# No tensor work on GpSimd: V laid out by head dimension for both pairs, Sinkhorn and P's transposes rearranged

## The chip, the core and the metric

The kernel runs on one core of a Trainium2 chip. The core's engines work in parallel, each through its own instructions in order: TensorE (PE; its weight loads are shown apart as PEld), VectorE (DVE), ScalarE (ACT), GpSimd (POOL) and SyncE (SP, which here only starts DMAs). The metric is the time of one execution on the device, in microseconds (us); lower is better.

## What is computed

Four batches of eight heads, 768 positions, head dimension 64. An 8 x 8 matrix per head is normalised by Sinkhorn steps and mixes the eight blocks of 96 positions of K and V; attention with the mixed K and V follows. Its output goes through a two-dimensional Fourier transform whose real part is added, and through a normalised MLP.

```python
def _attn_ref(q, k, v, sort_net):
    ...
    P = sort_net
    for _ in range(5):
        P = P - np.max(P, axis=-1, keepdims=True)
        P = np.exp(P)
        P = P / (np.sum(P, axis=-1, keepdims=True) + 1e-09)
        P = P / (np.sum(P, axis=-2, keepdims=True) + 1e-09)
    k_b = k.reshape(B, H, n_blocks, block, D)
    v_b = v.reshape(B, H, n_blocks, block, D)
    k_sorted = np.einsum('bhij,bhjcd->bhicd', P, k_b).reshape(B, H, S, D)
    v_sorted = np.einsum('bhij,bhjcd->bhicd', P, v_b).reshape(B, H, S, D)
    ...
    scores = scale * np.matmul(q_b, k_sb.transpose(0, 1, 2, 4, 3))
    scores = scores - np.max(scores, axis=-1, keepdims=True)
    attn = np.exp(scores)
    attn = attn / (np.sum(attn, axis=-1, keepdims=True) + 1e-09)
    return np.matmul(attn, v_sb).reshape(B, H, S, D).astype(np.float32)

def _moe_ref(x, w_ch1, w_ch2):
    X = np.fft.fft(x, axis=1)
    X = np.fft.fft(X, axis=2)
    mixed = np.real(X).astype(np.float32)
    u = x + mixed
    mu = np.mean(u, axis=-1, keepdims=True)
    var = np.mean((u - mu) ** 2, axis=-1, keepdims=True)
    un = (u - mu) / np.sqrt(var + 1e-06)
    ch = np.maximum(un @ w_ch1, 0.0) @ w_ch2
    return (u + ch).astype(np.float32)
```

## The kernel before

The kernel is one list of operations that a planner puts in order. `P.add` records an operation with the engines that may run it and a guessed cost on each, what it reads and writes, and a priority. `schedule` walks a simulated clock: each engine takes the ready operation of lowest priority number; where several engines may run one, the one that is free first takes it. The result is a fixed order on each engine, and an instruction that waits holds everything behind it on its engine. The guesses decide the order alone, not how long anything takes.

Inputs come by DMAs that GpSimd issues (line 395), small tables by SyncE. Sinkhorn (`sk`, lines 493 to 515) is a chain of 32-partition operations on VectorE with one exponential on ScalarE in each of five iterations. VectorE first clears the tiles `eb` and `ks` (437, 441). P is then spread out (`pk` at 517 on VectorE, `pv` at 521 on ScalarE) and transposed on TensorE: for the keys at 530, from which `bdk` is built (535, and `make_bdk` at 551 for later batches), and for the values at 648, from which `bdv` is built (653). The transposes at 648 are eight fp32 matmuls recorded as one operation.

Attention (`attn`) goes over pairs of heads: `q_copy` (771) gathers q into `qr`, `kqt` mixes the keys (786), copies them out to `ks` and transposes q into `qt` (807, 812), `scores` computes scores (830), their exponential into `ex` (839) and the exponential minus one into `eb` (851 on VectorE, 853 on ScalarE; one of three `ex` buffers is held until then), `av` multiplies with the mixed values and normalises (870 to 884). Copies out of PSUM and others go through one helper, `copy`, so many rows carry its line, 560, and are told apart by their tiles.

The values are handled for two pairs of batches, t = 0 and 1. `v_path` sums V over a block on TensorE (575) and makes the mean `vb`/`vbn` on VectorE (582 to 591). For t = 0 four copies of 1536 values (597) put V into the tile `vcx` with the head dimension innermost. `v_mix` then takes, for each of 64 dimensions d, the columns of `vcx` with that d as weights (626, a stride of 64 values) and subtracts the mean with a second matmul (628). For t = 1 GpSimd subtracts the mean in eight operations (607), which write `vcx` with d outermost: neighbours in the order of writing lie 96 values, 192 bytes, apart. The weights of a dimension then lie in a row (632) and no second matmul is needed. The mixed values go from PSUM into `vsf` (640).

`a_path` computes small tables `rr` (689 to 740). `dft1` and `dft2` are the Fourier transform; `y` is copied out of PSUM on ScalarE (941) and `yr`, its reversal, is made on VectorE or GpSimd (947). `dft2` also makes the normalisation, whose small steps at 1015 to 1024 run on GpSimd. `mlp` is the MLP: FF1 at 1067, its ReLU on ScalarE or VectorE (1079, 1076), FF2 at 1088, the sum at 1096, the store at 1099. Attention of a batch and the MLP of an earlier one are interleaved by their priorities.

```python
vcd = vcx[:, 0:6144].rearrange("p (d r c) -> p c r d", r=6, c=16)
for n in range(8):
    P.add({"POOL": (1.7, 1.8)},
          lambda _, n=n: nc.gpsimd.tensor_tensor(
              vcd[:, 2 * n:2 * n + 2],
              n3[:, 12 * n:12 * n + 12, :].rearrange(
                  "p (c r) d -> p c r d", r=6),
              vbn[:, None, None, :].broadcast_to([128, 2, 6, D]),
              op=ALU.subtract),
```

## Time and profile before

| | |
|---|---|
| median of 3 runs | 346.91 us (346.67 to 347.95) |
| the profiled execution | 349.38 us, span of the profile 347.6 us |
| TensorE busy | 287.0 us (83%) |
| VectorE busy | 216.0 us (62%) |
| ScalarE busy | 149.2 us (43%) |
| GpSimd busy | 90.4 us (26%) |
| chain that ended last | PE 66%, DVE 26%, issue 3%, POOL 2%, ACT 2% |

An engine's busy time counts its instructions from start to end, so one that is held up after it has started counts as busy. The span in 40 slices of 8.7 us (busy tenths of each engine):

```profile
PE   0397989777950009998999999999999999999994
DVE  7766889999999994297981559642552423531002
ACT  2364046755840006375892175054174162270520
POOL 8343601534289992000120023000022010010000
```

Rows of the list of groups read: line, engine, operation, out<-in, shapes, count | busy us, mean ns of one | idle before it, and what ended that. Rows of the timeline read: start, length, engine, line, operation, count [idle before it].

### The profile page before, as it was taken

How to read it: one execution, taken by the hardware profiler on the slowest of the kernel's cores; microseconds unless marked ns; L12 is line 12 of the kernel's file. 1: busy time of each engine (PE TensorE's matmuls, PEld its weight loads, DVE VectorE, ACT ScalarE, POOL GpSimd, SP SyncE). 2: the span in 40 equal slices, each digit the busy share in tenths (PEclk: the TensorE clock that was granted, in tenths of full speed). 3: DMA queues.
4: the chain of work that ended last, by engine and by line, in shares of the span. 5: the costliest groups of instructions: out<-in, count | busy, mean ns of one | idle time of the engine just before them, and what ended most of it. 6: DMA issues, size and time to landing. Idle time of an engine off the chain costs nothing.

```text
span 347.6 us, 6040 instructions
## 1 busy us (share of the span) xinstructions
PE 287.0 (83%) x2452; PEld 182.2 (52%) x2452; DVE 216.0 (62%) x404; ACT 149.2 (43%) x304; POOL 90.4 (26%) x103
## 2 busy tenths in 40 slices
PE   0397989777950009998999999999999999999994
PEld 0367978654630005575665566555565565564541
DVE  7766889999999994297981559642552423531002
ACT  2364046755840006375892175054174162270520
POOL 8343601534289992000120023000022010010000
PEclk9996965996995557998999999999999999999999
DMA  8999999630000009010000110100110100201002
GB/s 134 202 284 211 209 211 208 98 52 10 0 2 0 0 1 180 18 46 1 32 2 2 61 42 2 62 30 2 60 42 2 60 32 10 82 2 60 32 0 91
DMA packets 16402, 22.40 MB, mean 64 GB/s; under 512 B 1162, under 2 KB 11928, under 8 KB 16372
## 3 DMA queue, kind: packets, MB, share of 16 engines
q0 software_dynamic: 12144, 15.16, 24.6%
q1 hardware_dynamic: 4230, 6.85, 5.3%
q8 instruction: 19, 0.31, 0.4%
q14 instruction: 9, 0.07, 0.1%
HBM read 28.95 MB, written 6.29 MB: 101 GB/s over the span
## 4 chain that ended last, share of the span: by engine, by line
PE 66%; DVE 26%; issue 3%; POOL 2%; ACT 2%; DVEq 0%
PE bank L1088 24%; PE bank L1067 21%; DVE yr L947 9%; PE bank L870 3%; PE bank L626 3%; PE bank L987 2%; PE bank L786 2%; PE bank L1047 2%; DVE qt L560 1%; PE bank L628 1%; PE bank L575 1%; PE bank L830 1%; PE bank L807 1%; DVE rt L884 1%; PE bank L994 1%
## 5 line engine op out<-in xcount | busy, mean ns | idle before, releaser
L1067 PE MATMUL bank<-ut,w1sb 128*128 128x384 f16 x512 | 94.5, 330 | 0.0
L1079 ACT ACTIVATE hr<-bank 128x384 f16<-128x384 f32 x109 | 53.5, 491 | 85.4 <-PE bank L1067 82.7
L1088 PE MATMUL bank<-w2sb,hr 128*128 128x512 f16 x384 | 88.7, 381 | 0.0
L1067 PEld LDWEIGHTS <-w1sb 128*128 128x128 f16 x512 | 48.6, 99 | 33.9 <-issue 1.8
L1096 DVE TENSOR_TENSOR u<-bank,u 128x512 f32<-128x512 f32 x24 | 16.5, 688 | 70.0 <-PE bank L1088 70.0
L1088 PEld LDWEIGHTS <-hr 128*128 128x128 f16 x384 | 37.1, 98 | 41.3 <-issue 0.3
L839 ACT ACTIVATE ex<-bank 96x384 f32<-96x384 f32 x64 | 28.0, 482 | 55.3 <-DVE eb L851 31.1
L786 PE MATMUL bank<-bdk,kq 128*64 128x128 f16 x192 | 13.6, 261 | 31.6 <-ACT ex L839 30.6
L947 DVE TENSOR_SCALAR yr<-y 128x384 f16<-128x384 f16 x7 | 33.9, 4837 | 0.5 <-ACT y L941 0.5
L1002 DVE SCALAR_TENSOR_TENSOR u<-rt,bank 128x512 f32<-128x512 f16 x24 | 16.1, 679 | 27.9 <-PE bank L994 27.9
L607 POOL TENSOR_TENSOR vcx<-kq,vbn 128x768 f16<-128x768 f16 x8 | 30.7, 4234 | 1.4 <-DVE vbn L588 1.4
L1015 POOL TENSOR_SCALAR mv<-mv 128x3 f32<-128x3 f32 x8 | 3.1, 383 | 102.6 <-DVE mv L1010 102.5
L786 PEld LDWEIGHTS <-kq 128*64 128x64 f16 x192 | 9.1, 129 | 35.4 <-issue 34.4
L853 ACT ACTIVATE eb<-ex,negone 96x384 f16<-96x384 f32 x37 | 21.9, 612 | 0.3
L870 PE MATMUL bank<-vsf,eb 97*128 97x65 f16 x384 | 18.0, 207 | 1.5 <-issue 0.9
L560 DVE CAST vsf<-bank 96x512 f16<-96x512 f32 x22 | 16.6, 781 | 3.8 <-PE bank L628 3.1
L947 POOL TENSOR_SCALAR yr<-y 128x384 f16<-128x384 f16 x9 | 10.8, 1209 | 29.6 <-ACT y L941 29.6
L807 PE MATMUL bank<-pack,qr 128*128 128x128 f16 x96 | 9.1, 244 | 10.9 <-DVE qr L771 10.8
L870 PEld LDWEIGHTS <-eb 97*128 97x128 f16 x384 | 16.3, 106 | 3.4 <-issue 1.3
L771 POOL COPY qr<-kq 128x768 f16<-128x768 f16 x8 | 6.5, 826 | 44.2 <-PE bank L807 40.4
L884 DVE TENSOR_TENSOR rt<-bank,rz 128x384 f16<-128x384 f32 x32 | 17.4, 551 | 0.5
L1008 DVE BATCH_NORM_STATS2 st<-u 128x6 f32<-128x512 f32 x24 | 16.2, 687 | 0.4
(120 smaller groups left out, 406.6 us busy)
## 6 DMA issues: line engine op xcount, KB each, us to landing
out_dram<-u SPq DMA_DIRECT2D x24, 256.0 KB, 2.0
kq<-in_k_dram POOLq DMA_DIRECT2D x8, 384.0 KB, 7.8
kq<-in_q_dram POOLq DMA_DIRECT2D x8, 384.0 KB, 9.9
w1sb<-in_moe_w_ch_dram POOLq DMA_DIRECT2D x4, 512.0 KB, 15.3
w2sb<-in_moe_w_ch_dram POOLq DMA_DIRECT2D x4, 512.0 KB, 19.0
hr<-in_v_dram POOLq DMA_DIRECT2D x2, 768.0 KB, 11.5
kq<-in_v_dram POOLq DMA_DIRECT2D x2, 768.0 KB, 21.6
cs<-k_cs POOLq DMA_DIRECT2D x1, 579.0 KB, 15.7
```

The lines of the kernel that those rows point to most:

```text
L560: (nc.scalar.copy if e == "ACT" else V.tensor_copy)(dst, src)
L607: lambda _, n=n: nc.gpsimd.tensor_tensor(vcd[:, 2 * n:2 * n + 2], n3[:, 12 * n:12 * n + 12, :].rearrange("p (c r) d -> p c r d", r=6), vbn ...
L786: nc.tensor.matmul(ps.ap[64 * h2:64 * h2 + 64, 128 * r3:128 * r3 + 128], k16[:, 2 * hl + h2, 3 * half + r3, :], bdk[:, 2 * hp + h2].rearra ...
L839: nc.scalar.activation(ex.ap, pss[h2].ap[0:96, 0:384], AF.Exp, scale=SCALE),
L853: nc.scalar.activation(ed, src, AF.Identity, bias=negone[0:96])
L870: nc.tensor.matmul(po.ap[:, 65 * T:65 * T + 65], eb.ap[:, e0:e0 + 128], vsf[:, vi:vi + 65], start=(n == 0), stop=(n == 1), skip_group_chec ...
L884: P.add({"DVE": (0.45, 0.56)}, lambda _: V.tensor_tensor(rt.ap[:, :, D * h:D * h + D], po3()[:, :, 0:D], rz.ap[:, :, None].broadcast_to([1 ...
L947: nc.gpsimd).tensor_scalar(
L1067: nc.tensor.matmul(ps.ap[:, 0:GT], w1sb[:, c, 128 * fc:128 * fc + 128], ut.ap[:, c, :], start=(c == 0), stop=(c == 3))
L1079: nc.scalar.activation(hr[g][:, fc, :], ps.ap[:, 0:GT], AF.Relu)
L1088: nc.tensor.matmul(ps.ap, hr[g][:, fc, 128 * tt:128 * tt + 128], w2sb[:, fc, :], start=(fc == 0), stop=(fc == 15))
L1096: V.tensor_tensor(u.ap, ps.ap, u.ap, op=ALU.add),
```

## The change

- The clearing of `eb` and `ks` goes from VectorE to GpSimd, behind the first loads.
- In `sk` the exponentials are remembered. The first q copy must run on ScalarE and after the last exponential; the other q copies run on ScalarE or VectorE, none on GpSimd. The first `qt` copy runs on ScalarE.
- `make_bdk` and `yr` run on VectorE alone, the small `pmt` copy on ScalarE alone.
- V goes into `vcx` with d outermost for both pairs. For t = 0 eight copies of 768 values on VectorE or ScalarE do it; for t = 1 eight subtractions on VectorE. `v_mix` takes weights in a row in both cases, 128 columns wide except for the last dimension; for t = 0 the matmul with the mean stays.
- V's sum and copies for t = 0 wait for their half of the staging buffer's earlier readers only.
- P's eight fp32 transposes are recorded singly, so that others can go between them.
- The last `rr` operation goes over its halves one after the other, so it writes in a row and reads every second value.

```diff
     for n in range(4):
-        P.add({"DVE": (0.45, 0.5)}, lambda _, n=n: nc.vector.memset(
-            eb4[0:96, n, :], 0.0), w=[("ebz", n)], prio=-501.0, tag="ebz")
+        P.add({"POOL": (0.8, 0.9)}, lambda _, n=n: nc.gpsimd.memset(
+            eb4[0:96, n, :], 0.0), w=[("ebz", n)], prio=-190.0, tag="ebz")
...
+    exps = []
     def sk(c, fn):
-        P.add(c, fn, r=["pw", "rs"] + hk(1), w=["pw", "rs"], tag="sink")
+        o = P.add(c, fn, r=["pw", "rs"] + hk(1), w=["pw", "rs"], tag="sink")
+        if "ACT" in c:
+            exps.append(o)
...
-        P.add({"DVE": (1.15, 1.21), "POOL": (2.4, 2.5)}, f,
+        P.add({"DVE": (1.15, 1.21)}, f,
               r=["tkh", "pack"], w=[("bdk", 0), ("bdk", 1)], tag="mbdk")
...
-            P.add(pe(mm(512, 6) * (1.0 if t else 1.6)), f,
-                  r=[("nat", t, hf), "pack"] + stage, w=[psm], tag="psm")
+            P.add(pe(mm(512, 6) * (1.0 if t else 1.2)), f,
+                  r=[("nat", t, hf), "pack"] + (
+                      stage if t else stage[8 * hf:8 * hf + 8]), w=[psm], tag="psm")
...
-        if t == 0:
-            vcp = vcx[:, 0:6144].rearrange("p (r c d) -> p c r d", r=6, d=D)
-            for hf in range(4):
-                P.add({"DVE": dve(1536, 4.0), "ACT": act(1536, 0.1)},
...
-        else:
-            vcd = vcx[:, 0:6144].rearrange("p (d r c) -> p c r d", r=6, c=16)
-            for n in range(8):
-                P.add({"POOL": (1.7, 1.8)},
-                      lambda _, n=n: nc.gpsimd.tensor_tensor(
...
+        vcd = vcx[:, 0:6144].rearrange("p (d r c) -> p c r d", r=6, c=16)
+        for n in range(8):
+            src = n3[:, 12 * n:12 * n + 12, :].rearrange(
+                "p (c r) d -> p c r d", r=6)
+            dst = vcd[:, 2 * n:2 * n + 2]
+            if t == 0:
+                P.add({"DVE": dve(768), "ACT": act(768, 0.05)},
+                      lambda e, dst=dst, src=src: copy(e, dst, src),
+                      r=[("nat", 0, n // 4)] + stage[8 * (n // 4):8 * (
+                          n // 4) + 8], w=[("vcx", n)], tag="vcp")
+            else:
+                P.add({"DVE": dve(768)},
+                      lambda _, dst=dst, src=src: V.tensor_tensor(
+                          dst, src, vbn[:, None, None, :].broadcast_to(
+                              [128, 2, 6, D]), op=ALU.subtract),
                       r=[("nat", 1, n // 4), "vbn"] + stage,
-                      w=[("vcx", n2) for n2 in range(4)], tag="vcd")
+                      w=[("vcx", n)], tag="vcd")
...
-                    o = ps.ap[0:128 if t else 96, 128 * dd:128 * dd + 128]
+                    m = 96 if d == D - 1 else 128
+                    o = ps.ap[0:m, 128 * dd:128 * dd + 128]
+                    nc.tensor.matmul(o, vcx[:, 96 * d:96 * d + m], bd,
+                                     start=True, stop=(t == 1))
                     if t == 0:
-                        nc.tensor.matmul(o, vc3[:, 0:96, d], bd, start=True,
-                                         stop=False)
                         nc.tensor.matmul(
-                            o, vbn[:, d:d + 1].broadcast_to([128, 96]), bd,
+                            o, vbn[:, d:d + 1].broadcast_to([128, m]), bd,
                             start=False, stop=True)
-                    else:
-                        nc.tensor.matmul(o, vcx[:, 96 * d:96 * d + 128], bd)
...
-        def f(_):
-            for i in range(NB):
-                nc.tensor.matmul(
-                    ps.ap[:, 32 * i:32 * i + 32], pv[:, i, :],
-                    idf[0:32, 0:32])
-        P.add(pe(2.4), f, r=["pv", "pack"] + hk(1), w=[ps], tag="bdv")
+        for i in range(NB):
+            P.add(pe(0.3), lambda _, i=i: nc.tensor.matmul(
+                ps.ap[:, 32 * i:32 * i + 32], pv[:, i, :], idf[0:32, 0:32]),
+                r=["pv", "pack"] + hk(1), w=[ps], tag="bdv")
...
-            rr[0:64, 1, :].rearrange("p (n m) -> p m n", n=2),
-            hi2.ap[0:64, 0:512].rearrange("p (m n) -> p m n", n=2),
-            nlo[0:64], px.ap[0:64].rearrange("p (m n) -> p m n", n=2),
+            rr[0:64, 1, :].rearrange("p (n m) -> p n m", n=2),
+            hi2.ap[0:64, 0:512].rearrange("p (m n) -> p n m", n=2),
+            nlo[0:64], px.ap[0:64].rearrange("p (m n) -> p n m", n=2),
...
-        c = {"DVE": (0.28, 0.35)}
-        if b > 0:
-            c["POOL"] = (1.1, 1.2)
...
+        first = b == 0 and hp == 0
+        c = {"ACT": (0.7, 0.8)}
+        if not first:
+            c["DVE"] = (0.28, 0.35)
+        P.add(c, lambda e: copy(
+            e, qr.ap.rearrange("p r (h d) -> p r h d", h=2), src),
+            r=[("kq", slot["q", b, hf])], w=[qr], tag="qcp",
+            after=[exps[-1]] if first else [])
...
-        P.add({"DVE": (0.85, 0.95), "ACT": act(768, 0.0, 0.1)},
-              lambda e: copy(
+        c = {"ACT": act(768, 0.0, 0.0)}
+        if b or hp:
+            c["DVE"] = (0.85, 0.95)
+        P.add(c, lambda e: copy(
...
-                P.add({"DVE": (0.17, 0.26), "POOL": (0.7, 0.8)},
-                      lambda e: (V if e == "DVE" else
-                                 nc.gpsimd).tensor_scalar(
+                P.add({"DVE": (0.17, 0.26)}, lambda _: V.tensor_scalar(
```

What the planner makes of it is shown at three places. A row is an instruction as it stands on its engine: the line (the two kernels number them differently, each by its own file), the operation, out<-in, the shape written.

The first place is VectorE just before Sinkhorn's end and up to V's mean, for the first pair. In the kernel before (505 to 513 are Sinkhorn's steps, 517 spreads P, 535 builds `bdk`, 560 with `vcx` are V's copies):

```order
L513 TENSOR_TENSOR hr_72<-hr_72 32x64
L517 CAST hr_72<-hr_72 32x1024
L535 TENSOR_TENSOR bdk<-bank_66,pack 128x512 x2
L653 TENSOR_TENSOR bdv_0_115<-bank_67,pack 128x128
L560 CAST ks_76<-bank_63 128x3x8x16
L560 CAST ks_76<-bank_65 128x3x8x16
L560 COPY vcx<-hr_71 128x4x6x64 x3
```

In the changed kernel, where 508 to 516 are Sinkhorn's steps, 520 spreads P, 538 builds `bdk`, 562 is the copy helper and 585 V's mean:

```order
L516 TENSOR_TENSOR hr_72<-hr_72 32x64
L520 CAST hr_72<-hr_72 32x1024
L562 COPY vcx<-hr_71 128x2x6x64 x2
L538 TENSOR_TENSOR bdk<-bank_67,pack 128x512 x2
L562 CAST ks_77<-bank_64 128x3x8x16
L562 CAST ks_77<-bank_61 128x3x8x16
L562 COPY vcx<-hr_71 128x2x6x64 x3
L585 TENSOR_REDUCE vb<-bank_66 128x64
```

Two of V's copies now stand ahead of `bdk`, and three ahead of the mean, where three longer copies stood behind the first key copies.

The second place is ScalarE at the same time, in the changed kernel. 506 is Sinkhorn's exponential, 524 spreads P for the values; `qr` is a q copy, `qt` a copy of transposed q, `ks` a key copy:

```order
L506 ACTIVATE hr_72<-hr_72 32x64 x4
L562 COPY qr_78<-kq 128x768
L506 ACTIVATE hr_72<-hr_72 32x64
L562 COPY qr_79<-kq 128x768
L562 COPY qt_81<-bank_62 128x768
L524 COPY hr_72<-hr_72 32x1024
L562 COPY vcx<-hr_71 128x2x6x64 x2
L547 CAST tkh<-bank_67 128x256
L562 CAST ks_76<-bank_63 128x3x8x16
```

A q copy of another pair of heads than the first stands ahead of the fifth exponential, and two of V's copies ahead of the first key copies. On VectorE one `qt` copy still stands between the fourth and the fifth iteration.

The third place is VectorE around V's mean for the second pair. Before (560 with `vsf` are the mixed values' copies):

```order
L588 TENSOR_SCALAR vbn<-vb 128x64
L591 COPY vb<-vb 128x64
L1076 TENSOR_SCALAR hr_71<-bank_66 128x384
L947 TENSOR_SCALAR yr_97<-y_93 128x384
L851 TENSOR_SCALAR eb_75<-ex_83 96x4x96
L851 TENSOR_SCALAR eb_75<-ex_84 96x4x96
...
L551 TENSOR_TENSOR bdk<-tkh,pack 128x1024
L1096 TENSOR_TENSOR u_99<-bank_67,u_99 128x512
L560 CAST vsf<-bank_62 96x128x4
```

In the changed kernel (608 is the subtraction, 943 the reversed copy, 850 the exponential minus one, 553 `bdk`, 1092 the MLP's sum):

```order
L591 TENSOR_SCALAR vbn<-vb 128x64
L594 COPY vb<-vb 128x64
L608 TENSOR_TENSOR vcx<-kq,vbn 128x2x6x64
L943 TENSOR_SCALAR yr_97<-y_93 128x384
L850 TENSOR_SCALAR eb_75<-ex_84 96x4x96
...
L553 TENSOR_TENSOR bdk<-tkh,pack 128x1024
L608 TENSOR_TENSOR vcx<-kq,vbn 128x2x6x64 x7
L1092 TENSOR_TENSOR u_99<-bank_67,u_99 128x512
L1092 TENSOR_TENSOR u_100<-bank_68,u_100 128x512
L562 CAST vsf<-bank_63 96x128x4
```

The eight subtractions stand on VectorE itself, one ahead of the reversed copies and seven ahead of the mixed values' copies.

More of the change, by code (lines that the diff above doesn't have):

```diff
@@ L334 @@
     vcx = ct("vcx", [128, 128 * D], F16)
-    vc3 = vcx.rearrange("p (c d) -> p c d", d=D)
     dtab = vcx[:, 6144:7168].rearrange("p (c w) -> p c w", c=4)
@@ L549, in f @@
         def f(e):
-            g = V if e == "DVE" else nc.gpsimd
-            g.tensor_tensor(
+            V.tensor_tensor(
                 bdk, tkh[:, :, 8 * b:8 * b + 8].rearrange("p i h -> p h i")[
@@ L902, in dft1 @@
                 tag="pmt")
-        P.add({"ACT": (0.17, 0.22), "POOL": (0.2, 0.3)},
-              lambda e: (nc.scalar.copy if e == "ACT" else
-                         nc.gpsimd.tensor_copy)(
+        P.add({"ACT": (0.17, 0.22)},
+              lambda _: nc.scalar.copy(
                   pmt[:, :, DM:DM + 1], pmt[:, :, 0:1]),
```

24 lines of the change are left out of this document (5 added, 19 removed).

## Prediction

> **What bounds the kernel now.** I read the busy digits of the page first. From about 99 to 130 us TensorE and ScalarE stand at 0 while VectorE and GpSimd stand at 9, so something holds the whole core there. The view by windows, the list of waits and the chain of work that ended last say what.
>
> ```profile
> 100.00:110.00 10.00, 0.31 (x6) 0.24 (x4) 10.00 (x1) 0.00 (x0) 10.00 (x4) 0.72 0.00 0
> ACT ex L839 <- DVE eb L851: 31.1, 2, 30.3
> PE bank L786 <- ACT ex L839: 30.6, 2, 30.1
> ```
>
> In ten microseconds VectorE runs one instruction and GpSimd four; TensorE is idle because ScalarE has no buffer, and ScalarE because VectorE doesn't come to L851. The timeline shows that instruction and what goes with it (start, length, engine, line).
>
> ```profile
> 98.86 30.75 DVE L947 TENSOR_SCALAR yr<-y 128x384 f16<-128x384 f16 x1
> ...
> 98.46 30.70 POOL L607 TENSOR_TENSOR vcx<-kq,vbn 128x768 f16<-128x768 f16 x8 [1.38 <-DVE vbn L588]
> ...
> 130.44 1.19 PE L786 MATMUL bank<-bdk,kq 128*64 128x128 f16 x12 [30.13 <-ACT ex L839]
> ...
> 131.76 0.25 DVE L947 TENSOR_SCALAR yr<-y 128x384 f16<-128x384 f16 x1
> ...
> 145.69 2.58 PE bank L632 x44
> ```
>
> A reversed copy on VectorE that takes 0.25 us at 131.76 starts just after the eight centring operations on GpSimd and ends with them. I cut the run into four stages: up to the end of the first V mix (44.6 us), from there to this copy (98.86), from it to the second V mix (145.69, so 46.8 us), and the rest. By the written order 64 FF1 matmuls and 28 FF2 matmuls come before the second mix in the kernel before, 64 and 32 in the changed one, so the stages can be compared.
>
> **The price of a scattered write.** In the changed kernel sixteen operations write 768 half-precision values each, every one 192 bytes from the one before: eight copies for the first pair (five on VectorE, three on ScalarE by the order) and eight subtractions on VectorE for the second. No row of before shows this on VectorE at this stride; these are nearest.
>
> ```profile
> L740 DVE SCALAR_TENSOR_TENSOR rr<-qt,pack,bank 64x512 f16<-64x512 f16 x2 | 5.0, 2482 | 0.0
> L607 POOL TENSOR_TENSOR vcx<-kq,vbn 128x768 f16<-128x768 f16 x8 | 30.7, 4234 | 1.4 <-DVE vbn L588 1.4
> L443 POOL MEMSET vsf<- 96x128 f16 x1 | 0.7, 739 | 0.0
> L560 DVE CAST vsf<-bank 96x512 f16<-96x512 f32 x22 | 16.6, 781 | 3.8 <-PE bank L628 3.1
> L560 ACT CAST vsf<-bank 96x512 f16<-96x512 f32 x10 | 6.7, 787 | 7.9 <-PE bank L632 5.8 <-PE bank L628 2.1
> L560 DVE CAST qt<-bank 64x512 f16<-64x512 f32 x1 | 0.7, 673 | 0.0
> L560 ACT CAST qt<-bank 64x512 f16<-64x512 f32 x1 | 0.6, 579 | 0.5 <-PE bank L707 0.5
> ```
>
> L740 writes alternately to two places 512 bytes apart and takes 2482 ns, although L1002 does the same kind of operation on 512 values, written in a row, in 679 (row below). L443 only writes, 128 values 130 bytes apart, in 739 ns. L607 takes 30.70/8 = 3.84 us each, 5.0 ns a value. The mixed V (vsf) is written four values at a time: two engines that differ by 94 ns on contiguous writes both come to 0.78 us there. So the writes set the pace, not the arithmetic. From start to start L740 is shorter:
>
> ```profile
> L1002 DVE SCALAR_TENSOR_TENSOR u<-rt,bank 128x512 f32<-128x512 f16 x24 | 16.1, 679 | 27.9 <-PE bank L994 27.9
> 59.67 2.48 DVE L740 SCALAR_TENSOR_TENSOR rr<-qt,pack,bank 64x512 f16<-64x512 f16 x1
> 61.77 0.75 DVE L730 SCALAR_TENSOR_TENSOR rr<-qt,pack,bank 128x129 f16<-128x129 f16 x2
> ```
>
> That is 2.10 us for 512, 4.1 ns a value, so **3.15 us for 768**. I take this for all sixteen, as the only scattered operation of VectorE. Bounds: 0.9 us (a plain 679 ns scaled to 768 values) and 4.23 us (L607's whole mean).
>
> The Trainium skill's "SBUF — State Buffer", section "Door 1: The DMA port swizzle", says that accesses within a 16-byte line run at full rate and each step to a new line pays; it names no amount, and L740's 2482 ns agrees. Its "VectorE: DVE Perf Modes", "Mode 1× (REGULAR) — the baseline", gives one result per cycle for odd strides as well, an estimated 0.80 us for 768; by that the time would be that of the cheap-write rival below, and L740 speaks against it.
>
> **Third stage, where the gain is.** The GpSimd block goes, and with it the stall. VectorE now does one subtraction, then the reversed copies and what waited behind them, then seven subtractions in a row, and only then the second mix. The small work is read from where the kernel before does it:
>
> ```profile
> 129.53 0.61 DVE L851 TENSOR_SCALAR eb<-ex 96x384 f16<-96x384 f32 x2
> ...
> 132.04 1.02 DVE L560 CAST ks<-bank 128x384 f16<-128x384 f32 x2
> ...
> 133.54 1.22 DVE L551 TENSOR_TENSOR bdk<-tkh,pack 128x1024 f16<-128x1024 f16 x1
> ```
>
> From 129.53 to 134.76 is 5.2 us; the changed order has two more key copies (1.0) and one more reversed copy (0.25): 6.5. With 8 x 3.15 = 25.2 that makes 31.7 us in place of 46.8: **-15.1**. TensorE's own work there, 130.44 to 145.69 = 15.3 us, lies beside it and isn't the bound unless a subtraction costs under (15.3 - 6.5)/8 = 1.1 us.
>
> **First stage.** These rows carry it.
>
> ```profile
> 4.27 0.15 DVE L498 TENSOR_REDUCE hr<-hr 32x8 f32<-32x64 f32 x1
> ...
> 12.30 0.96 DVE L560 COPY qt<-bank 128x768 f16<-128x768 f16 x1 [0.33 <-PE bank L807]
> ...
> 14.64 0.68 DVE L517 CAST hr<-hr 32x1024 f16<-32x1024 f32 x1
> 15.80 0.69 DVE L535 TENSOR_TENSOR bdk<-bank,pack 128x512 f16<-128x512 f32 x1 [0.48 <-PE bank L530]
> ...
> 20.97 1.77 DVE L560 COPY vcx<-hr 128x1536 f16<-128x1536 f16 x3
> ...
> 27.32 0.94 DVE L560 COPY qt<-bank 128x768 f16<-128x768 f16 x1
> ...
> 9.52 0.53 POOL L395 DMA_DIRECT2D tab<-k_tab  x1 [1.24 <-DMA kq<-in_q_dram]
> ...
> 19.28 1.49 PE L786 MATMUL bank<-bdk,kq 128*64 128x128 f16 x24
> ...
> 30.08 0.34 PE L628 MATMUL bank<-bdv,vbn 128*96 128x128 f16 x1 [1.75 <-DVE vbn L588]
> ```
>
> The memsets leave VectorE, so Sinkhorn can start before 4.27. But ScalarE's first q copy now stands ahead of the fifth exponential and waits for q, which lands at about 9.5 (GpSimd's wait for it ends there). A qt copy of 0.96 still stands ahead of the fifth iteration. Copy 9.5 to 10.3, transposes to 11.0, qt copy to 11.9, the last iteration 1.4 (before: from 13.26, the end of the qt copy, to the cast at 14.64), the cast 0.7: it ends at 14.0 instead of 15.3. Sinkhorn isn't undisturbed, and 1.3 us is won.
>
> Then two scattered V copies stand ahead of bdk, which can start at 14.0 + 6.3 = 20.3 instead of 15.8 (+4.5). Three more stand ahead of the V mean: 9.45 instead of 1.77 (+7.7). Splitting P's transposes lets the key matmuls start when the first half of bdk ends: before it ended at 16.49, and they began at 19.28 (-2.8). Two qt copies, that at 27.32 and one like it, go to ScalarE (-1.9). The memsets on GpSimd lie under its waits for loads, and cost nothing while those last. The mix then starts at 30.1 + 7.5 = 37.6.
>
> The mix itself gets contiguous weights. Its weight loads now, and its last matmul:
>
> ```profile
> 40.08 0.24 PEld L626 LDWEIGHTS <-vcx 128*96 128x96 f16 x1
> 40.23 0.14 PEld L628 LDWEIGHTS <-vbn 128*96 128x96 f16 x1
> 40.30 0.24 PEld L626 LDWEIGHTS <-vcx 128*96 128x96 f16 x1
> ...
> 44.63 0.22 PE L628 MATMUL bank<-bdv,vbn 128*96 128x128 f16 x1
> ```
>
> A pair takes 0.15 + 0.07 us by starts; L632, contiguous, ran 44 in 2.58, 0.06 each. So 0.06 + 0.07 = 0.13 a pair, 64 pairs 8.3 us, against 14.5 (30.08 to 44.6): -6.2. The output copies, 16 by 0.78 on two engines, fit under that. Stage: 7.5 - 6.2 = **+1.3**. If the mean's loads cost twice as much at 128 columns, it is 4.5 more.
>
> **Second and fourth stage.** The windows of both (length; TensorE, weight loads, VectorE, ScalarE, GpSimd busy), and two rows:
>
> ```profile
> 50.00:98.86 48.86, 42.67 (x534) 31.78 (x531) 46.55 (x106) 34.68 (x74) 17.10 (x24) 0.83 0.44 76
> 150.00:340.00 190.00, 187.63 (x1405) 108.53 (x1403) 90.93 (x186) 87.11 (x178) 16.48 (x30) 0.99 0.08 30
> ...
> 70.60 1.63 DVE L947 TENSOR_SCALAR yr<-y 128x384 f16<-128x384 f16 x1
> L689 DVE COPY qt<-bank 64x128 f32<-64x128 f32 x8 | 2.0, 278 | 0.4 <-PE bank L668 0.4
> ```
>
> In the second, VectorE is busy 46.55 of 48.86 us, so its work counts. Off it go L740's stride (2.10 to about 0.6: -1.5), the blocked copy at 70.60 (-1.3) and four of L689's copies, which now stand ahead of the mix (-1.1). To it come five reversed copies from GpSimd (+1.25) and one bdk, 1.22 at 133.54 above. Sum **-1.5**. In the fourth TensorE is busy 187.63 of 190, so at most 2.4 can go; the second L740, shortened by 1.5, stands there: **-1.5**. ScalarE takes q copies at 0.8 each; it is busy 34.68 of 48.86 in the second stage and its idle time covers them.
>
> **Sum.** 1.3 - 1.5 - 15.1 - 1.5 = -16.8. The profiled execution took 349.38 (span 347.6), giving 332.6; it stands 0.7% above the median of the runs, 346.91, on which it is **330.1**.
>
> **Rivals.**
> 1. One-input copies write through two paths. L517 handles 1024 values in 0.68, twice L1002's rate, so VectorE's five copies might cost 1.6 us each. Then ScalarE's copies bound the first stage, about 5 us sooner: 325. For it, L517; against, nothing scattered in the trace runs at that rate. The Trainium skill's "VectorE: DVE Perf Modes", "What auto-detection actually checks", allows two ports to a one-source copy whose outermost size is even, as here; no run here shows it for scattered writes.
> 2. Cheap writes, 0.9 us each, if L740's two alternating places are a special case. In the first stage bdk starts as before, three copies cost 0.9 more, and -2.8 - 1.9 - 6.2 stand: -10; in the third TensorE's 15.3 bounds: -31.5. With the others -44.5: 302. Against it stand L740, L443 and both vsf rows.
> 3. Costlier writes. Each us on one operation costs 8 in the third stage and 5 in the first. At 5.0 ns a value, 3.84 us, it is 13 x 0.7 = 9 more: 339; at L607's mean, 4.23, 344.
> 4. Slower than before: the same mechanism beyond 3.15 + 16.8/13 = 4.4 us, 5.8 ns a value, where the stall merely comes back as VectorE's own work. At 5 us it gives 354. L607's 4.23 is the most that the trace shows, though with two engines' contention.
>
> That the change fails of its word (Sinkhorn) is in the sum.
>
> **How the numbers follow.** Forecast 0.45 (324 to 336), rival 1 0.20, rival 2 0.12, rival 3 0.15, rival 4 0.08. A measurement tells 0.5% from no change. Faster takes all but rival 4 and a few parts of rival 3: 0.88; same 0.04, slower 0.08. The range 303 to 341 leaves out half of rival 2, the top of rival 3 and rival 4.
>
> **What would show it.** The subtractions' mean on VectorE: near 3.2 us right, under 1.2 rival 2, over 4.5 rival 4. The copies' mean tells rival 1. TensorE's gap before the second mix should be some 16 us, the first mix should start near 38 and last 8. The reversed copies should all take 0.25. The forecast is wrong if VectorE isn't what TensorE waits for ahead of either mix.

## The result, and the profile after

| | before | after |
|---|---|---|
| median | 346.94 us (346.67 to 347.95, 4 runs) | 334.16 us (333.02 to 335.87, 4 runs) |
| profiled execution, span | 349.38, 347.6 | 334.09, 332.3 |

The ratio is 0.963, 95% interval 0.9585 to 0.9676: faster. Here and below a ratio compares fast runs alone, which leaves out two of the six runs of one version, rows_firstold. Cut where the prediction cuts, the view by windows of the changed kernel gives (stretch; its length; TensorE, weight loads, VectorE, ScalarE and GpSimd busy with their counts; granted clock, DMA share, GB/s):

```profile
0.00:33.78 33.78, 16.95 (x137) 10.91 (x137) 25.76 (x60) 24.69 (x30) 31.94 (x37) 0.96 1.08 209
33.78:42.67 8.89, 8.89 (x127) 8.89 (x127) 7.35 (x15) 6.46 (x10) 1.08 (x2) 0.78 1.09 210
42.67:94.38 51.71, 44.51 (x615) 32.88 (x614) 48.81 (x119) 38.97 (x83) 7.15 (x12) 0.93 0.57 100
94.38:132.07 37.69, 15.20 (x104) 7.56 (x102) 36.95 (x27) 7.12 (x16) 2.35 (x3) 0.74 0.23 32
132.07:332.30 200.23, 194.85 (x1476) 114.72 (x1476) 96.05 (x200) 91.59 (x184) 10.98 (x25) 0.99 0.11 36
```

The cuts are the start of the first mix, of its last matmul, of the first subtraction and of the second mix. The second stage of the kernel before, by the same view:

```profile
44.60:98.86 54.26, 47.16 (x607) 35.49 (x607) 50.67 (x117) 36.76 (x78) 17.21 (x24) 0.81 0.52 89
```

| stage | before | after | change | forecast |
|---|---|---|---|---|
| 1, to the end of the first mix | 44.6 | 42.7 | -1.9 | +1.3 |
| 2, to the second pair's V | 54.3 | 51.7 | -2.6 | -1.5 |
| 3, to the second mix | 46.8 | 37.7 | -9.1 | -15.1 |
| 4, the rest | 201.9 | 200.2 | -1.7 | -1.5 |
| sum | | | -15.3 | -16.8 |

These are differences of two profiled executions. The medians lie 12.8 us apart: the profiled execution of the kernel before, with a mean granted clock of 0.910, took 349.38 us, 2.4 more than its median.

In the third stage VectorE is busy for 36.95 of 37.69 us, and TensorE for 15.20. The timeline (start, length, engine, line; idle before it):

```profile
94.38 3.97 DVE L608 TENSOR_TENSOR vcx<-kq,vbn 128x768 f16<-128x768 f16 x1
97.93 0.51 DVE L943 TENSOR_SCALAR yr<-y 128x384 f16<-128x384 f16 x1
...
105.16 26.85 DVE L608 TENSOR_TENSOR vcx<-kq,vbn 128x768 f16<-128x768 f16 x7
...
105.28 7.07 PE L1084 MATMUL bank<-w2sb,hr 128*128 128x512 f16 x32
132.07 5.88 PE L624 MATMUL bank<-bdv,vcx 128*128 128x128 f16 x64 [19.73 <-DVE vcx L608]
```

The stall at the reversed copy is gone: yr (L943) follows the first subtraction at once, 3.55 us after its start. The seven others take 26.85 us in a row, and TensorE, done with its feed-forward matmuls at 112.35, waits 19.73 us for the last. The eight take 3.55 + 26.85 = 30.4 us of VectorE, nearly what GpSimd's eight took before (30.70). The wait changed its owner.

### The profile page after: what moved, and what is told of

Same layout as the page of the kernel before. It is cut to its first block, busy times and chain, and to the rows that moved or that the text cites. A ratio compares the mean times of both kernels' runs of the same rounds, so it can differ in the third digit from the quotient of the medians.

```text
span 332.3 us, 6040 instructions
## 1 busy us (share of the span) xinstructions
PE 280.4 (84%) x2452; PEld 175.0 (53%) x2452; DVE 214.9 (65%) x416; ACT 168.8 (51%) x320; POOL 53.5 (16%) x79
## 4 chain that ended last, share of the span: by engine, by line
PE 66%; DVE 21%; ACT 5%; DMA 4%; issue 2%; POOL 1%; DVEq 0%; POOLq 0%
PE bank L1063 25%; PE bank L1084 24%; DVE vcx L608 7%; DMA out_dram<-u 2%; ACT vcx L562 2%; PE bank L869 2%; PE bank L930 2%; PE bank L983 2%; DMA kq<-in_q_dram 2%; DVE rt L883 2%; PE bank L1043 2%; DVE vcx L562 2%; PE bank L829 1%; PE bank L624 1%; PE bank L627 1%
## 5 line engine op out<-in xcount | busy, mean ns | idle before, releaser
L1063 PE MATMUL bank<-ut,w1sb 128*128 128x384 f16 x512 | 95.7, 330 | 0.0
L1092 DVE TENSOR_TENSOR u<-bank,u 128x512 f32<-128x512 f32 x24 | 16.7, 700 | 59.3 <-PE bank L1084 59.3
L624 PE MATMUL bank<-bdv,vcx 128*128 128x128 f16 (+1 forms) x128 | 14.9, 263 | 20.5 <-DVE vcx L608 19.7
L608 DVE TENSOR_TENSOR vcx<-kq,vbn 128x768 f16<-128x768 f16 x8 | 30.8, 4186 | 0.0
L562 ACT CAST vsf<-bank 96x512 f16<-96x512 f32 x17 | 13.1, 790 | 29.5 <-PE bank L624 26.8
L624 PEld LDWEIGHTS <-vcx 128*128 128x128 f16 (+1 forms) x128 | 13.0, 123 | 20.2 <-DVE vcx L608 20.2
L869 PE MATMUL bank<-vsf,eb 97*128 97x65 f16 x384 | 16.3, 195 | 1.1 <-ACT vsf L562 0.9
L829 PE MATMUL bank<-qt,ks 64*128 64x96 f16 x256 | 12.7, 213 | 5.3 <-DVE u L998 1.9
L783 PE MATMUL bank<-bdk,kq 128*64 128x128 f16 x192 | 11.6, 248 | 6.4 <-DVE ks L562 3.1
L869 PEld LDWEIGHTS <-eb 97*128 97x128 f16 x384 | 14.5, 98 | 3.8 <-issue 1.2
L394 POOL DMA_DIRECT2D kq<-in_k_dram x8 | 6.4, 803 | 54.5 <-DVE vcx L608 38.9
```

The costliest lines, as they stand in the source:

```text
L562: (nc.scalar.copy if e == "ACT" else V.tensor_copy)(dst, src)
L608: lambda _, dst=dst, src=src: V.tensor_tensor(dst, src, vbn[:, None, None, :].broadcast_to([128, 2, 6, D]), op=ALU.subtract),
L624: nc.tensor.matmul(o, vcx[:, 96 * d:96 * d + m], bd, start=True, stop=(t == 1))
L869: nc.tensor.matmul(po.ap[:, 65 * T:65 * T + 65], eb.ap[:, e0:e0 + 128], vsf[:, vi:vi + 65], start=(n == 0), stop=(n == 1), skip_group_chec ...
L1063: nc.tensor.matmul(ps.ap[:, 0:GT], w1sb[:, c, 128 * fc:128 * fc + 128], ut.ap[:, c, :], start=(c == 0), stop=(c == 3))
L1092: V.tensor_tensor(u.ap, ps.ap, u.ap, op=ALU.add),
```

## The experiments

Each ratio is to the kernel before, on the same chip in the same set of runs. Over the sets the median of the kernel before was 346.9 to 348.2 us, so times from different sets agree to some 0.4%.

### The stall alone

Theory: in the kernel before, VectorE is kept out by GpSimd's operations, and those last so long because of their scattered writes. Rival: the copy waits for something else. The first kernel leaves the eight operations out, and with them the layout of the second pair's V:

```diff
-            for n in range(8):
-                P.add({"POOL": (1.7, 1.8)}, lambda _, n=n: nc.gpsimd.tensor_tensor(
-                    vcd[:, 2 * n:2 * n + 2], ...
+            P.add({"POOL": (0.2, 0.3)}, lambda _: nc.gpsimd.tensor_tensor(
+                vcx[:, 0:64], vbn, vbn, op=ALU.subtract), ...
```

> The kernel before, with the eight subtractions on GpSimd left out; one of 64 values stands in their place, so V of the second pair is not laid out and its part of the output is not the reference's. Theory (VectorE's reversed copy at 98.86 us stood still for 30.7 us only because GpSimd's row of two-input operations held VectorE out of it): it takes 0.25 to 0.5 us and starts at its time, and the time falls by 28 to 36 us, to 311 to 319. Rival (it waited for its own inputs or for a buffer that the second pair sets free): a wait of over 10 us stays at that place, and the time stays above 330.

314.86 us (313.99 to 316.69), ratio 0.9059 (0.8999 to 0.912). The reversed copy, VectorE's timeline:

```profile
96.05 0.25 DVE L941 TENSOR_SCALAR yr<-y 128x384 f16<-128x384 f16 x1
```

The theory held. Some 33 us hang on those eight operations. The whole change, which keeps their work, gained 12.8.

### The same work on GpSimd, written side by side

Each operation takes eight dimensions of all rows instead of twelve rows of all dimensions. The values written together in time now lie together in memory.

```diff
-            vcd = vcx[:, 0:6144].rearrange("p (d r c) -> p c r d", r=6, c=16)
+            vcd = vcx[:, 0:6144].rearrange("p (d r c) -> p d r c", r=6, c=16)
...
-                          vcd[:, 2 * n:2 * n + 2],
-                          n3[:, 12 * n:12 * n + 12, :].rearrange("p (c r) d -> p c r d", r=6),
+                          vcd[:, 8 * n:8 * n + 8],
+                          n3[:, :, 8 * n:8 * n + 8].rearrange("p (c r) d -> p d r c", r=6),
```

> The kernel before, with its eight subtractions still on GpSimd and in the same place of every engine's order, but writing side by side (eight dimensions of all rows each, read 768 bytes apart). Theory (VectorE's reversed copy stands still for as long as GpSimd's row of operations lasts, and how long that is follows from the writes): each takes 1.6 to 2.2 us in place of 3.84, the row 13 to 18, the reversed copy stands for just as long, and the time falls by 13 to 18 us, to 329 to 335. Rival A (the copy is let through between two of GpSimd's operations once these are short, as in the kernel of prices, where a copy was let through after the first of four): the copy takes under 3 us, the time is 314 to 322, since then only the second mix waits. Rival B (reading 768 bytes apart is as dear on GpSimd as the writes were): no change, 345 to 349.

323.09 us (322.93 to 324.32), ratio 0.9285 (0.9252 to 0.9317). GpSimd's row and what VectorE does beside it:

```profile
96.73 16.29 POOL L607 TENSOR_TENSOR vcx<-kq,vbn 128x768 f16<-128x768 f16 x8 [1.37 <-DVE vbn L588]
...
97.13 1.58 DVE L947 TENSOR_SCALAR yr<-y 128x384 f16<-128x384 f16 x1
98.64 3.92 DVE L851 TENSOR_SCALAR eb<-ex 96x384 f16<-96x384 f32 x2
...
104.81 1.90 DVE L947 TENSOR_SCALAR yr<-y 128x384 f16<-128x384 f16 x1
```

The writes do set the length: the row takes 16.29 us in place of 30.70. But the theory's time fell, and rival A's mechanism held, its 322 missed by one: VectorE is let in between two operations and held up again at each such instruction, 1.6 to 2 us a time in the rows shown, rather than once for 16. Work that stayed on GpSimd, with other writes alone, beats the change by 11 us.

### When GpSimd lets go

A kernel of single operations: VectorE starts one while GpSimd runs a row. The comments are added here.

```diff
+            beside(row, 4, back)    # 768 values side by side; reversed copy
+            beside(wide, 4, back)   # the kernel's scattered subtraction
+            beside(wide, 8, back)
+            beside(wide, 4, both)   # single-precision copy
+            beside(sets, 3, cast)   # memsets; cast as L520
```

> Single operations only; the output holds none of the reference's values. VectorE starts one short operation while GpSimd runs a row of its own. Alone, the reversed half-precision copy of 384 values should take 0.25 us, the cast of 1024 values 0.68, a copy of 384 single-precision values 0.3. Theory (GpSimd keeps VectorE out until the end of its row where its writes are 192 bytes apart, as in the kernel before; where they are side by side VectorE comes in after one operation, as in the kernel of prices): beside four scattered subtractions the reversed copy takes some 15 us, beside eight some 31, beside four in a row 1.3 to 1.7. Rival (it comes in after one operation everywhere, and the stall of the kernel before had a further cause): about 3.9 us beside scattered ones, whether four or eight. Beside three memsets of 1536 values on GpSimd (1.36 us each), theory: the cast takes 1.8 to 2 us, as in the changed kernel; rival (the memsets do not touch it): 0.68.

The timeline, GpSimd's row and VectorE's operation by pairs, the first three lines being VectorE alone:

```profile
10.51 0.49 DVE L58 TENSOR_SCALAR sa<-sb 128x384 f16<-128x384 f16 x2
10.92 1.39 DVE L61 CAST sc<-src 32x1024 f16<-32x1024 f32 x2
12.24 0.73 DVE L64 TENSOR_SCALAR src<-src 128x384 f32<-128x384 f32 x2
...
13.45 6.76 POOL L52 TENSOR_TENSOR gd<-ga,gb 128x768 f16<-128x768 f16 x4
13.52 1.68 DVE L58 TENSOR_SCALAR sa<-sb 128x384 f16<-128x384 f16 x1
...
20.29 15.45 POOL L48 TENSOR_TENSOR dv<-ga,gb 128x768 f16<-128x768 f16 x4
...
20.44 15.41 DVE L58 TENSOR_SCALAR sa<-sb 128x384 f16<-128x384 f16 x1
...
36.18 30.70 POOL L48 TENSOR_TENSOR dv<-ga,gb 128x768 f16<-128x768 f16 x8
...
36.33 30.66 DVE L58 TENSOR_SCALAR sa<-sb 128x384 f16<-128x384 f16 x1
...
67.31 15.70 POOL L48 TENSOR_TENSOR dv<-ga,gb 128x768 f16<-128x768 f16 x4
...
67.46 4.07 DVE L64 TENSOR_SCALAR src<-src 128x384 f32<-128x384 f32 x1
...
82.67 4.92 POOL L55 MEMSET gd<- 96x1536 f16 x3
...
83.14 1.70 DVE L61 CAST sc<-src 32x1024 f16<-32x1024 f32 x1
```

The 30.7 us of the kernel before stand here by themselves: the copy comes in after the last of four or of eight scattered operations, but after the first of four whose writes lie side by side. A single-precision copy comes in after the first scattered one, at 4.07 us. The cast takes 1.70 us beside memsets, against 0.70 alone. So the theory held, but for the cast, 0.1 us under its 1.8 to 2. The kernel of the next section ends with four more such pairs, beside four side-by-side operations of 1.63 us each. There a half-precision copy took 1.30 us, one with two half-precision inputs 1.90 and a single-precision copy 1.70, each until GpSimd's first was done. A copy out of TensorE's output buffer took 0.55 and didn't wait. The expectation given with that kernel, that the half-precision copy stands still to the end of the row, failed.

### The price of a scattered write

256 values, written every s-th, each kind twice:

```diff
+            for s in (1, 2, 4, 8, 16, 32, 96):
+                for _ in range(2):
+                    V.tensor_tensor(every(dv, s), sa[:, 0:N], sb[:, 0:N], op=ALU.subtract)
```

> No attention at all, only single operations on 256 values a partition, each kind twice, whose lengths are read from the timeline (start to start); the output holds none of the reference's values. Written every s-th value (s = 1, 2, 4, 8, 16, 32, 96; 2 bytes each). Theory (what is paid for is each 16 bytes touched anew): VectorE with two inputs takes about 0.3 us at s = 1, a quarter of the full price at 2, half at 4, the full 4.9 ns a value, 1.25 us, from 8 on, the same at 96; runs of 8 or 16 side by side cost no more than s = 1; one input half of it, 0.64 us (2.5 ns a value, from 1.93 us for 768); ScalarE 4.9 to 5.1 ns a value; GpSimd as VectorE with two inputs. Rival A (any gap costs the full price): 1.25 us already at s = 2. Rival B (the price grows with the distance): 96 dearer than 32, 32 than 8. Reading every s-th value: 1.44 us for 768 in the kernel with writes side by side, so 0.5 us for 256 with two inputs and 0.3 with one; if reading were as dear as writing, 1.25. Last, four kinds of operations that VectorE starts while GpSimd runs a row of two-input ones: a half-precision copy between on-chip buffers is expected to stand still until GpSimd's row ends, as the reversed copy at 98.86 us did before; one that reads TensorE's output buffer, or whose operands are all in single precision with two inputs, to run at once.

Single rows of the timeline: two inputs at s = 1 and 96, one input at 96, then runs of four values 96 apart, then two inputs that read every 96th.

```profile
31.98 0.29 DVE L50 TENSOR_TENSOR dv<-sa,sb 128x256 f16<-128x256 f16 x1
...
42.90 1.44 DVE L50 TENSOR_TENSOR dv<-sa,sb 128x256 f16<-128x256 f16 x1
...
52.55 0.81 DVE L54 COPY dv<-sa 128x256 f16<-128x256 f16 x1
...
55.05 0.29 DVE L58 TENSOR_TENSOR dv<-sa,sb 128x256 f16<-128x256 f16 x1
...
60.34 0.59 DVE L65 TENSOR_TENSOR gd<-wide,sb 128x256 f16<-128x256 f16 x1
```

All strides by the same view, in us:

| written every s-th | 1 | 2 | 4 | 8 | 16 | 32 | 96 |
|---|---|---|---|---|---|---|---|
| VectorE, two inputs | 0.29 | 0.45 | 0.73 | 1.29 | 1.23 | 1.27 | 1.44 |
| VectorE, one input | 0.23 | 0.31 | 0.45 | 0.73 | 0.70 | 0.72 | 0.81 |
| ScalarE | 0.41 | 0.48 | 0.77 | 1.33 | 1.26 to 1.33 | 1.30 | 1.47 |
| GpSimd, two inputs | 0.67 | | 0.77 | 1.34 | 1.26 | | 1.47 |

From a step of 8 values (16 bytes) on, three engines pay the same 1.2 to 1.5 us, 4.8 to 5.8 ns a value; VectorE pays half of it where there is one input. The theory held for the steps in the main (0.45 and 0.73 us at 2 and 4 are more than its quarter and half); rivals A and B fell, but for the last tenth at 96. It didn't hold for runs: two side by side take 0.37 us and four 0.29, so a run of two is cheaper than a step of four, which touches as many 16-byte pieces. A count of the pieces is not the whole rule. Reading 96 apart costs 0.59 us with two inputs and 0.39 with one, less than half of writing so.

### Side by side on VectorE

The edit of the kernel on GpSimd above, in the changed kernel: for the second pair's subtractions alone, then for the first pair's copies too. Each operation then needs both halves of V.

> The changed kernel with the writes side by side and the reads 768 bytes apart for the eight subtractions of the second pair alone; the first pair's copies are as in the changed kernel. Theory (the third stage is set by the eight subtractions, 30 us of 37.7): subtractions of 0.9 to 1.7 us, the second mix starts 17 to 23 us earlier than at 132.1, and the time falls by 16 to 22 us, to 312 to 318. Then what separates this kernel from the one with both pairs changed is what the first pair's copies cost, by the trace 3 to 6 us. Rival (reads as dear as writes): within 3 us of 334.

> The changed kernel with one difference: each of the sixteen operations that lay V out handles eight of the 64 dimensions of all 96 rows instead of twelve rows of all dimensions, so that it writes its 768 values side by side and reads them 768 bytes apart. Theory (the price is that of writing values one by one, 192 bytes apart: 3.77 us for 768 values in the changed kernel's second pair, 1.93 for a copy on VectorE, 3.93 on ScalarE): the eight subtractions fall to 0.9 to 1.7 us each, the wait of TensorE before the second mix from 19.7 us to about 2, the copies to under 1 us, and the time from 334.2 to 305 to 316 us. Rival A (reading 768 bytes apart is as dear as writing 192 bytes apart): the subtractions stay at 3.5 us or more and the time is within 3 us of 334. Rival B (the subtractions get cheap, but the second pair's mix then waits for something else): subtractions under 1.7 us and the time above 322.

314.9 us (313.09 to 316.23), ratio 0.9041 (0.8986 to 0.9095); and with both **312.25 us** (311.82 to 313.03), ratio 0.8971 (0.8927 to 0.9014). With both, the copies' groups by line and the timeline:

```profile
L562 DVE COPY vcx<-hr 128x768 f16<-128x768 f16 x6 | 5.4, 934 | 0.0
L562 ACT COPY vcx<-hr 128x768 f16<-128x768 f16 x2 | 3.0, 1495 | 0.0
...
96.79 11.00 DVE L608 TENSOR_TENSOR vcx<-kq,vbn 128x768 f16<-128x768 f16 x8
...
104.16 1.50 PE L624 MATMUL bank<-bdv,vcx 128*128 128x128 f16 x24
...
108.43 1.84 PE L624 MATMUL bank<-bdv,vcx 128*128 128x128 f16 x17 [2.77 <-DVE u L1092]
```

Both times came as the theory had them. The eight subtractions take 11.0 us and 22 us more go than with the change. TensorE goes from a feed-forward matmul to the second mix without a wait, while the subtractions still run (to 107.79). Written side by side, the first of them fills whole dimensions, so the mix can start on these; scattered, each dimension needs all eight. After 24 matmuls TensorE waits 2.77 us for a sum (L1092) that stands behind the subtractions on VectorE: a rest of the old wait is left. The first pair's copies are worth 2.65 us by the medians, under the 3 to 6 expected, and the intervals of the two ratios overlap. ScalarE's two copies take 1.5 us each, where under 1 was expected.

### Parts of the change alone

Only the subtractions moved, in the kernel before:

```diff
-                P.add({"POOL": (1.7, 1.8)},
-                      lambda _, n=n: nc.gpsimd.tensor_tensor(
+                P.add({"DVE": dve(768)},
+                      lambda _, n=n: V.tensor_tensor(
```

> The kernel before with one part of the change alone: the eight subtractions of the second pair stand on VectorE instead of GpSimd, all else as it was (first pair in its old layout, Sinkhorn with the memsets, P transposes whole). Theory (that move is worth the third stage's 9.1 us, and part of the 2.5 of the second): subtractions at 3.7 to 3.8 us each, time 334 to 340 us, that is 7 to 13 us under 346.9. Rival (the gain came from the first pair's new layout and the undisturbed Sinkhorn, and the subtractions cost VectorE as much as they cost GpSimd): within 2 us of 346.9.

338.93 us (337.81 to 339.72), ratio 0.9732 (0.9683 to 0.9781). The theory held: this one line is worth 8 to 9 us. What of the other 5 is the first pair's new layout was asked with that undone in the changed kernel (four copies written side by side, `vc3[:, 0:96, d]` as weights):

```diff
-                    nc.tensor.matmul(o, vcx[:, 96 * d:96 * d + m], bd,
+                    nc.tensor.matmul(o, vcx[:, 96 * d:96 * d + m] if t
+                                     else vc3[:, 0:96, d], bd,
```

> The changed kernel with one part undone: the first pair's V laid out as in the kernel before (four copies that write side by side, weights of the first mix read 128 bytes apart). Theory (the new layout sped the mix up by 6 us and delayed its start by as much, through the dear copies): the first mix starts near 28 to 30 us, takes 14.5 to 16, ends at 43 to 45 in place of 42.7, and the time is 333 to 337. Rival (the layout of the first pair is what sets the changed kernel 4.8 us below the kernel before with the subtractions moved alone): 338 to 340.

333.33 us (332.11 to 334.43), ratio 0.9575 (0.9537 to 0.9613). Start of the first mix and of its last matmul, there and in the changed kernel:

```profile
28.05 0.27 PE L639 MATMUL bank<-bdv,vcx 128*96 128x128 f16 x1 [0.42 <-ACT bdv L563]
...
42.54 0.22 PE L643 MATMUL bank<-bdv,vbn 128*96 128x128 f16 x1
```

```profile
33.78 0.26 PE L624 MATMUL bank<-bdv,vcx 128*128 128x128 f16 x1 [0.73 <-DVE vcx L648]
...
42.67 0.22 PE L627 MATMUL bank<-bdv,vbn 128*96 128x128 f16 x1
```

The new layout gains 5.6 us in the mix and loses 5.7 ahead of it, with the scattered copies: nothing, as the theory had it. By elimination the 5 us come from the smaller edits together (reversed copies, the `rr` operation, transposes, memsets); no run shows the share of each.

The memsets put back on VectorE, in the changed kernel and in the version with all writes side by side:

```diff
-        P.add({"POOL": (0.8, 0.9)}, lambda _, n=n: nc.gpsimd.memset(
-            eb4[0:96, n, :], 0.0), w=[("ebz", n)], prio=-190.0, tag="ebz")
+        P.add({"DVE": (0.45, 0.5)}, lambda _, n=n: nc.vector.memset(
+            eb4[0:96, n, :], 0.0), w=[("ebz", n)], prio=-501.0, tag="ebz")
```

> The changed kernel with one part undone: the memsets stand on VectorE ahead of Sinkhorn again. Theory (moving them won 1.8 us at Sinkhorn's end and lost 1.16 at the cast that GpSimd's memsets hold up, so 0.6 us at the first stage, and ScalarE's copies of V hide even that): Sinkhorn ends near 14.6 us, the cast takes 0.68 again, bdk's first half starts 0 to 0.8 us later, the time is within 1.5 us of 334.2. Rival (the undisturbed Sinkhorn is worth the 1.8 us by which it ends sooner): 335.5 to 337.

> The version with writes side by side for both pairs, and the memsets on VectorE as in the kernel before. Theory (without the dear copies the first stage hangs on Sinkhorn, the cast and bdk, where moving the memsets wins 0.6 us net): 312 to 314, 0 to 1.5 us above 312.25. Rival (GpSimd's memsets delay its loads and the cast by more than VectorE's would cost): 309 to 312.

335.48 us (334.71 to 336.66), ratio 0.9641 (0.9611 to 0.9671), and 312.99 us (312.1 to 314.07), ratio 0.8984 (0.8954 to 0.9014). They lie 1.3 and 0.7 us above the kernels with the memsets on GpSimd (by the ratios 0.4 and 0.5), less than the intervals tell apart: the second as the theory had it, the first at the edge of theory and rival. VectorE there, and in the changed kernel:

```profile
14.21 0.73 DVE L520 CAST hr<-hr 32x1024 f16<-32x1024 f32 x1
...
18.41 0.94 DVE L538 TENSOR_TENSOR bdk<-bank,pack 128x512 f16<-128x512 f32 x1
23.35 0.69 DVE L538 TENSOR_TENSOR bdk<-bank,pack 128x512 f16<-128x512 f32 x1 [4.00 <-ACT tkh L547]
```

```profile
12.82 1.84 DVE L520 CAST hr<-hr 32x1024 f16<-32x1024 f32 x1
...
18.14 0.94 DVE L538 TENSOR_TENSOR bdk<-bank,pack 128x512 f16<-128x512 f32 x1
21.85 0.69 DVE L538 TENSOR_TENSOR bdk<-bank,pack 128x512 f16<-128x512 f32 x1 [2.78 <-ACT tkh L547]
```

The cast is 0.73 us again, and bdk's first half starts only 0.27 us later. The second half is 1.5 us later: it waits for ScalarE, whose two V copies started 1.5 us later, behind a copy that waits for Sinkhorn.

### Two more versions

Side by side for the second pair, old layout for the first:

> Writes side by side for the second pair's subtractions, and the first pair's V laid out as in the kernel before. Beside the version with the new layout and writes side by side for both (312.25 us) it tells what the first pair's new layout is worth where its copies are cheap. Theory (there the mix starts near 30 us and takes 8.7, against 14.5 from 28 in the old layout, so the first stage ends 3.7 us later; of such gains about half reached the end so far): 313.5 to 316. Rival (the second stage, bound by VectorE, takes up whatever the first gains): within 1 us of 312.25.

319.22 us (315.56 to 322.06), ratio 0.9122 (0.9076 to 0.9167), which stands for some 317.5 us: neither theory nor rival. Its six runs lie in three pairs, near 315.8, 319.2 and 322.0 us, the lowest pair inside the theory's range and all above the 312.25 us of the new layout. In the profiled execution, at 322.06 us, the first mix's last matmul started at 45.4 us, against 38.8 with the new layout; the theory had 3.7 us for this difference. With cheap copies the first pair's new layout is a gain, then; how large, and why the runs part so, stays open.

In the best version, the plan has each group of a mix wait only for the operations that write its dimensions:

```diff
-                  r=[("vcx", i) for i in range(8)] + [("bdv16", t)]
+                  r=[("vcx", n // 2)] + ([("vcx", n // 2 + 1)] if n % 2 and n < 15 else []) + [("bdv16", t)]
```

> The version with writes side by side for both pairs, and each group of four dimensions of a mix waiting only for the operations that write its own dimensions, in place of all eight. Theory (TensorE no longer waits for the subtractions, since feed-forward matmuls stand ahead of the second mix, and the first mix waits for the mixing matrix): within 1.5 us of 312.25. Rival (both mixes still start late because of the whole set): 307 to 310.

312.32 us (310.64 to 313.87), ratio 0.8968 (0.8936 to 0.9001): no change, as the theory's time had it. But the edit changes the order of the plan alone: on the chip the mix already started before the last subtraction was done, as shown above. In the new order it starts at 99.71 us, among the subtractions, and TensorE waits four times for a single one, 0.3 to 0.8 us each. So the run says that this order is worth nothing, and not what a wait for all eight would cost.

## Why the prediction was right, and where it was off

**The bound and the sign: right.** The block on GpSimd held the core (33 us without it), VectorE's own subtractions took its place, and the second mix waits for them, 19.7 us where some 16 were named.

**Third stage: the price of a scattered write was too low.** 3.15 us were taken from L740; measured are 30.4 us for eight, 3.80 each, that is 5.2 us more than the 25.2 of the sum. The small work between took 7.2 us (97.93 to 105.16) instead of 6.5. L740 was the wrong model: it writes to two places in turn and took 4.1 ns a value, where the subtractions take 5.0. GpSimd's row (3.84 each), whose mean was read as a price with two engines contending, was the plain price: the table of strides shows the same 1.44 to 1.47 us for 256 values on VectorE, ScalarE and GpSimd, each at work alone. That is rival 3's price, though not its time. The `vsf` rows were taken as a sign of the same thing, but in the table runs of four values cost nothing extra; why `vsf` was dearer than `qt` is open.

**First stage: the price of a copy was too high, and a wait was missed.** The groups by line:

```profile
L562 ACT COPY vcx<-hr 128x768 f16<-128x768 f16 x3 | 11.8, 4132 | 0.0
L562 DVE COPY vcx<-hr 128x768 f16<-128x768 f16 x5 | 9.9, 2241 | 0.0
```

VectorE's five copies took 9.9 us, not 15.8: the mechanism of rival 1, and with it ScalarE's copies (3.9 us each) became what bdk's second half waits for, as that rival had it. The mix started at 33.8 instead of 37.6 and took 8.9 us instead of 8.3. Its last wait, 0.73 us, was for its matrix `bdv` (L648) and not for the mean, which was there at 31.03. So the stage became 1.9 us shorter where the forecast had it 1.3 longer. The Trainium skill's "VectorE: DVE Perf Modes", "What auto-detection actually checks", allows two ports to a copy with one source; half the price for scattered writes, 0.81 against 1.44 us for 256 values, agrees with it.

**Memsets on GpSimd "cost nothing": wrong.** They lengthened the cast from 0.68 to 1.84 us. Sinkhorn ended at 12.8, but the cast only at 14.7, where 14.0 was forecast: 0.7 us won of the 1.3 in the sum. Whether even that reached the end no run shows, since the kernel with the memsets put back isn't told apart from this one.

**Second and fourth stage: near.** The `rr` operation and, all but one (0.51 us at 97.93), the reversed copies came as forecast:

```profile
L735 DVE SCALAR_TENSOR_TENSOR rr<-qt,pack,bank 64x512 f16<-64x512 f16 x2 | 1.5, 740 | 0.0
L943 DVE TENSOR_SCALAR yr<-y 128x384 f16<-128x384 f16 x16 | 4.2, 267 | 1.5 <-ACT y L939 1.4
```

In the second stage VectorE is busy 1.9 us less, of the 2.6 gained. The granted clock there was 0.81 before and 0.93 after; what that gives TensorE was not in the forecast, and no run separates it.

**The sum: near, partly by luck.** +6.0 in the third stage, -3.2 in the first, -1.1 and -0.2 in the others: 332.6 forecast in profiled time, 334.09 measured. Two prices were wrong in opposite directions, one for each number of inputs, and the first stage's error took away about half of the third's. The median is 4.1 us above its forecast: 1.5 from the sum, and 2.5 because the forecast took before's 0.7% between profile and median to hold after too, where the two agree (334.09 and 334.16).

**The rival not seen.** Cheap writes (302 us) were held to depend on the hardware; they depended on the order of the loop. The write price was read as that of the layout, though the same layout can be filled side by side, with the distance on the read: 312.25 us.

## What to carry to other kernels

Where a layout has to be turned round on an engine, put the distance on the read and write side by side: here 11 us instead of 30 for the same result, on the same engine. An operation that blocks another engine should be made short before it is moved: moved, it took as long on its new engine. Read a price from an operation of the same number of inputs on the same pattern, and look for a second row of another engine at that stride; if they agree, the write is the likely cause.

## What was not expected of the hardware

- GpSimd kept VectorE's half-precision reversed copy out for its whole row where its writes were scattered (15.41 us beside four, 30.66 beside eight), and for one operation where they were not (1.68). The Trainium skill's "SBUF — State Buffer", "Who interferes with whom", says that whoever issues first has the shared ports for the whole instruction; here it was eight instructions. Why a single-precision copy got in after one scattered operation (4.07) is open.
- Half-precision values written one by one at steps of 16 to 192 bytes cost some 5 ns each (1.2 to 1.5 us for 256) on VectorE (two inputs), ScalarE and GpSimd alike, and about half of that for a copy on VectorE. On VectorE, runs of four, 192 bytes apart, cost nothing extra (0.29 us).
- Two issues of loads by GpSimd, in the changed kernel, lasted until the row of copies that VectorE ran beside them was done: the first until 18.70 us, the copies until 18.57; the second until 29.43, the copies until 29.30. It isn't bound to scattered writes: in the version that writes side by side an issue that stands beside three of the copies (to 20.99 us) lasts 2.97 us too. No run separates the cause. The timelines of the two:

```profile
14.01 4.69 POOL L394 DMA_DIRECT2D cs<-k_cs  x1
...
23.25 6.18 POOL L394 DMA_DIRECT2D w1sb<-in_moe_w_ch_dram  x1
```

```profile
18.33 2.97 POOL L394 DMA_DIRECT2D kq<-in_k_dram  x1 [1.22 <-DMA kq<-in_k_dram]
```
